# Chunked attention into a mixture of experts on one core: an earlier load of the second pair's first q and k, and another order of its softmax steps

## The chip, the cores and the metric

The kernel runs on one core of a Trainium2 chip. The metric is the device time of one execution, in microseconds (us); 1496.49 us is the median of three runs before the change. An engine executes its own instructions in the order of its own queue: TensorE (PE in the profile, PEld for its weight loads), VectorE (DVE), ScalarE (ACT), GpSimd (POOL) and SyncE (SP), which in this kernel issues every DMA. Engines wait for each other by semaphores.

## What is computed

The reference has two parts, and the second reads what the first writes:

```python
# attention inside chunks of 64 positions (8 batches, 8 heads, 576 positions, head_dim 64)
scores = scale * np.matmul(q_c, k_c.transpose(0, 1, 2, 4, 3))
scores = scores - np.max(scores, axis=-1, keepdims=True)
attn = np.exp(scores)
attn = attn / (np.sum(attn, axis=-1, keepdims=True) + 1e-09)
out = np.matmul(attn, v_c)
# the result as 4608 tokens of 512, through 4 experts of 512 -> 1024 -> 512
p = domain_probs / (domain_probs.sum(-1, keepdims=True) + 1e-09)
for e in range(E):
    h = np.maximum(x @ w1[e], 0.0)
    out += p[:, e:e + 1] * (h @ w2[e])
```

All of it is in fp32; the kernel splits each factor of the expert products into a high and a low part of type fp32r and adds three products of parts.

## The kernel before

The 4608 tokens are nine blocks of 512. The first block is worked alone, the other eight as four pairs of blocks. A pass takes one block or pair through half of one expert (512 of the 1024 hidden columns), so there are eight passes to each block or pair and 40 in all, numbered n = 0 to 39. Pass 0 is `startup`, passes 1 to 7 are `plain_pass`, pass 8 is `first_later_pass`, passes 9 to 39 are `later_pass`. The products of a pair follow a scheme with seven products in place of eight (`Group`, `LaterGroup`, `Outer`, L742 to L954). In `later_pass` a pass has 28 steps, listed in `WOVEN`; each step is one product of six matmuls of 128x512 on PE. Steps named g and h make hidden values of this pass; steps named a and b multiply the hidden values of the pass before with the second weight matrix. The products a1, a6, a7, a4 accumulate in one PSUM bank, and after each of them DVE adds the bank to an accumulator in SBUF (L923); the next product of the bank waits for that add. b1, b6, b7, b4 do the same after them, in the same bank.

What happens beside the products is written out by hand: `add(at, i, f)` puts f behind step i (counted from 0), and everything is emitted in this order, so the order in the code is the order in each engine's queue. The attention of a pair is done during the passes of the pair before it, two tiles of 128 tokens (t and t + 1) at a time. For the second pair `attend_second` does it, in passes 8 to 13:

- `both_load` (L248) loads q and k of two tiles into the tile hf3, two DMAs of 512 KB. The first call is in the last plain pass (n = 7, step 6, L1450), the others at step 26 of passes 9 to 11. In pass 7 the stores `keep(0)` (L488) read the former content of hf3.
- `two_next` multiplies weights and v of the two tiles before (L228) and makes the scores of the next two (L209, 64 matmuls of 64x64), at step 5 in passes 10 to 12 and at step 1 in pass 8.
- `a_softmax` is, for one tile, the maximum and its subtraction on DVE (L263, L268) and the exponential on ACT (L274).
- `two_weights` is five DVE instructions: the sums (L277), a small constant (L278), the reciprocal (L280), the scaling (L284) and a transpose in 32x32 blocks (L155).
- `a_place` is five copies on ACT (L161, L165), which put the transposed blocks in place.
- `two_load_v` loads v of the two tiles.

Other work that DVE does beside it: the hidden values (L896, L861), sums of hidden values for the seven products (L867, some on POOL), and sums of parts of the first weight matrix (L513). ACT and POOL make high parts (L873, L530) and low parts (L876, L531).

SP's queue holds the loads of weights for a ring of buffers (`ring_load`, L588), stores (L460, L488, L534, L1001), loads of raw weights (`half_load`, L508), and the loads named above. A DMA waits in this queue until its buffer is free and until the DMA eight places ahead of it has landed.

Of the kernel before, what the change touches and what calls it, by code (L numbers as in the profile page):

```python
# [18 lines left out]
NT = SUB // P  # L19
# [6 lines left out]
PAIR = 2  # L26
# [5 lines left out]
def chunk_attention_moe(ctx: ExitStack, tc: tile.TileContext, qk, v, v0, dp, w1, w2, out):  # L32
# [105 lines left out]
    def a_less_max(t):  # L138
        less_max(st[t]["sc"])

    def a_exps(t):
        a_exp(st[t]["sc"])

    def a_softmax(t):
        a_less_max(t)
        a_exps(t)

    def a_scale(t):

        s = st[t]  # L150
        s["e"] = att.tile([P, 2, HG, C], F32, name="e")
        scale(s["e"], s["sc"], s["r"])

    def a_transpose(t):
        nc.vector.transpose(st[t]["sc"], st[t]["e"])  # L155

    def a_place(t, name="pt"):

        s = st[t]
        s["pt"] = att.tile([P, 2, HG, C], F32, name=name)  # L160
        nc.scalar.copy(out=s["pt"], in_=s["sc"])  # L161
        for half in range(2):
            for i in range(2):
                here, there = (slice(half * C + k * B, half * C + (k + 1) * B) for k in (i, 1 - i))
                nc.scalar.copy(  # L165
                    out=s["pt"][there, :, :, i * B : (i + 1) * B],
                    in_=s["sc"][here, :, :, (1 - i) * B : (2 - i) * B],
                )
# [42 lines left out]
    def two_sums(t, name=None):  # L211
        z = bank(name)[:, : 2 * HG].rearrange("p (c j) -> p c j", c=2)
        st[t]["r"] = inverse_sums(st[t]["sc"], z)

    def two_weights(t):
        two_sums(t, "B1")
        a_scale(t)
        a_transpose(t)
# [29 lines left out]
    def both_load(t):  # L248

        both = hf_tile(3, (2, 2, 2, HG, C), F32)  # L250
        for i in range(2):
            st[t + i] = {"x": both[:, i]}
            nc.sync.dma_start(out=both[:, i], in_=qk[t + i].rearrange("g c d x h s -> (c d) g x h s"))
# [91 lines left out]
    def hf_tile(j, shape=(2, 2, SUB), dtype=F32R):  # L345

        return hpool.tile([P, *shape], dtype, name=f"hf{j}")

    def of_pass(w, n):
        return w[n % n_pass // 2, n % 2]  # L350
# [146 lines left out]
    def pieces(i, n):  # L497
        return scratch[0][:, SUB + 2 * i * P : SUB + 2 * (i + n) * P].rearrange(
            "p (a b c) -> p a b c", b=2, c=P
        )  # L500

    def half_load(n, g, fs=(0, 1)):
        if not scratch:
            scratch.append(xpool.tile([P, NK * PAIR * SUB], F32, name="xraw"))
        for f in fs:
            cols = slice((2 * f + g) * P, (2 * f + g + 1) * P)
            to = pieces(7 * g + AT[f"a{f + 1}1"], 2)
            nc.sync.dma_start(out=to.rearrange("p a b c -> p (a b) c"), in_=of_pass(w1, n)[:, :, cols])  # L508
# [390 lines left out]
    class Outer:  # L899
# [17 lines left out]
        def add(self, src, i, s):  # L917
            key = self.n // n_pass, 2 * i + self.g + NK * s
            if key not in acc:
                acc[key] = opool.tile([P, SUB], F32, name=f"acc{key[1]}")  # L920
                nc.scalar.copy(out=acc[key], in_=src)
            else:
                nc.vector.tensor_tensor(out=acc[key], in0=src, in1=acc[key], op=ALU.add)  # L923
# [456 lines left out]
    def plain_pass(n, beside, xs):  # L1380

        at, last_pass = {}, n == n_pass - 1
# [64 lines left out]
        for r, i in ((0, 2), (1, 2), (2, 3), (3, 5), (4, 5)):  # L1447
            add(at, i, lambda r=r: ring_load(0, r, (RINGS[0] + RINGS[1])[r]))
        add(at, 1, lambda: probs_load(n + 1, 0), lambda: probs_load(n + 1, 1))
        add(at, 6, lambda: half_load(n + 2, 0), lambda: both_load((1 + PAIR) * NT))  # L1450
        add(at, 6, lambda: ring_load(0, 5, RINGS[1][2]))
        issue(steps[:-1], at, beside, True)
        return steps[-1], w2_do("keep_sums")
# [82 lines left out]
    def attend_second(at, n):  # L1536

        t0, r = (1 + PAIR) * NT, n - n_pass - 1
        t = t0 + 2 * max(r, 0)
        if r < 0:  # L1540
            add(at, 1, lambda: two_next(None, t))
            add(at, 2, lambda: a_softmax(t))
            add(at, 3, lambda: two_weights(t), lambda: a_less_max(t + 1))
            add(at, 5, lambda: a_exps(t + 1))
            add(at, 7, lambda: a_place(t))
            return
        if r > 4:
            return
        if r:
            add(at, 5, lambda: two_next(t - 2, t if r < 4 else None, ("B1", "C0")))  # L1550
        if r == 4:
            return
        if r:
            add(at, 6, lambda: a_softmax(t))
            add(at, 12, lambda: two_weights(t))
            add(at, 13, lambda: a_softmax(t + 1))
            add(at, 15, lambda: a_place(t))
        for i in range(2):
            for odd in range(2):
                add(at, (7 if r else 14) + 2 * i + odd, lambda i=i, odd=odd: two_load_v(t + i, i, odd))  # L1560
        add(at, 18, lambda: two_weights(t + 1))
        add(at, 22, lambda: a_place(t + 1, "e"))
        if r < 3:
            add(at, 26, lambda: both_load(t + 2))

# [76 lines left out]
    def later_pass(n, ahead, late, held):  # L1642
# [39 lines left out]
        if 0 < pair < n_pairs - 1:  # L1682
            attend_two(at, pair + 1, n % n_pass)
        elif pair == 0:
            attend_second(at, n)
# [206 lines left out]
```

## Time and profile before

| what | us |
|---|---|
| median of three runs | 1496.49 |
| the three runs | 1496.47, 1496.91, 1496.49 |
| the profiled execution: its own time | 1496.58 |
| the profiled execution: its span, first to last instruction | 1494.5 |
| busy in the span: PE, DVE, POOL, ACT | 1463.3, 1080.8, 975.1, 624.1 |

Three stretches of the span, from the view that sums busy time by stretch (us):

| stretch | length | PE | DVE | POOL | ACT |
|---|---|---|---|---|---|
| 232.1 to 275.9 (pass 9) | 43.8 | 42.90 | 37.15 | 39.23 | 25.19 |
| 370.4 to 418.2 (pass 12) | 47.8 | 42.88 | 36.80 | 32.42 | 21.21 |
| 456.3 to 494.4 (a pass without attention) | 38.1 | 38.10 | 27.78 | 34.95 | 16.51 |

The profile is one execution. Its timeline merges equal instructions that follow each other; a bracket at a row's end gives the idle time of that engine before the row and what ended it. The granted clock of PE is 1.00 at 2.4 GHz and 0.50 at 1.2 GHz. Some matmul records can be missing, and the ends of matmuls are modelled. A wait for several semaphores is put down to the one that came last.

### The profile page before, as it was taken

The page shows a single profiled execution, that of the slowest core. Times are in us where ns is not written, and L with a number is a line of the kernel's source. Part 1 is how long each engine was busy: PE and PEld are TensorE (multiplying, and loading weights), DVE is VectorE, ACT ScalarE, POOL GpSimd, SP SyncE. Part 2 cuts the span into 40 slices and gives each one's busy share as a digit, 9 for nine tenths or more (in the row PEclk, how much of TensorE's full clock was granted, in tenths as well). Part 3 has the DMA queues.
Part 4 walks back from the last instruction along what each step waited for, and adds up shares of the span by engine and source line. Part 5 has one row for each costly group of instructions (what it writes and reads, how often), then busy time and mean ns, then how long its engine had stood idle before and what let it go on. Part 6 is the DMA issues. An engine that isn't in the chain of part 4 may idle for free.

```text
span 1494.5 us, 23390 instructions
## 1 busy us (share of the span) xinstructions
PE 1463.3 (98%) x8574; PEld 1203.3 (81%) x8574; DVE 1080.8 (72%) x1500; ACT 624.1 (42%) x1169; POOL 975.1 (65%) x728
## 2 busy tenths in 40 slices
PE   9999979988899999999999999999999999999998
PEld 7888867776688888888888888888888888888887
DVE  6666738787778797778766886777768866666666
ACT  5566525444444343444432434444333343333232
POOL 6878858776679875555555755555657655555554
PEclk9999989999999999999999999999999999999999
DMA  9899676856667879776655679676565696565655
GB/s 317 319 334 327 228 283 222 283 204 218 243 213 244 298 241 259 246 240 235 202 196 192 219 218 290 225 233 204 193 198 197 202 258 204 192 207 191 205 195 155
DMA packets 198418, 348.51 MB, mean 233 GB/s; under 512 B 70160, under 2 KB 109344, under 8 KB 197920
## 3 DMA queue, kind: packets, MB, share of 16 engines
q1 hardware_dynamic: 198304, 347.02, 70.6%
q8 instruction: 68, 1.11, 0.3%
q14 instruction: 46, 0.38, 0.1%
HBM read 275.59 MB, written 71.38 MB: 232 GB/s over the span
## 4 chain that ended last, share of the span: by engine, by line
PE 88%; DVE 4%; POOL 3%; DMA 2%; ACT 1%; issue 1%; SPq 0%; POOLq 0%; ACTq 0%; DVEq 0%
PE A L698 46%; PE C L698 25%; PE B L698 14%; POOL hf L876 2%; PE psa L209 1%; PE B L228 1%; DMA hf<-in_qk 1%; DMA v_in<-in_v 1%; DVE wraw L867 1%; DVE xraw L513 1%; POOL hf L388 0%; DMA w<-hf 0%; DVE acc L923 0%; DVE e L284 0%; POOL wraw L867 0%
## 5 line engine op out<-in xcount | busy, mean ns | idle before, releaser
L876 POOL TENSOR_TENSOR hf<-wraw,hf 128x512 fp32r<-128x512 f32 x384 | 505.6, 1334 | 254.2 <-ACT hf L873 251.1
L698 PE MATMUL A<-hf,wf 128*128 128x512 f32 x1536 | 395.4, 393 | 14.5 <-DVE acc L923 14.5
L698 PE MATMUL A<-xh,wf 128*128 128x512 f32 (+1 forms) x1120 | 388.2, 390 | 0.0
L698 PEld LDWEIGHTS A<-hf,wf 128*128 128x128 f32 x1536 | 286.6, 188 | 79.8 <-DVE acc L923 20.3
L873 ACT CAST hf<-wraw 128x512 fp32r<-128x512 f32 x384 | 233.4, 622 | 278.5 <-DVE wraw L867 98.0
L698 PEld LDWEIGHTS A<-xh,wf 128*128 128x128 f32 x1120 | 210.7, 188 | 45.0 <-POOL wf L531 0.5
L761 ACT COPY s<-A 128x512 f32<-128x512 f32 x192 | 112.8, 587 | 299.4 <-PE A L698 298.7
L698 PE MATMUL A<-xl,wf 128*128 128x512 f32 (+1 forms) x560 | 218.0, 389 | 0.0
L923 DVE TENSOR_TENSOR acc<-A,acc 128x512 f32<-128x512 f32 x232 | 157.9, 681 | 76.5 <-PE A L698 76.2
L698 PE MATMUL C<-xh,wf 128*128 128x512 f32 (+1 forms) x584 | 201.1, 388 | 1.0 <-DVE B L896 1.0
L698 PE MATMUL C<-hf,wf 128*128 128x512 f32 x768 | 195.6, 390 | 0.0
L698 PEld LDWEIGHTS C<-hf,wf 128*128 128x128 f32 x768 | 145.0, 189 | 30.3
L698 PEld LDWEIGHTS C<-xh,wf 128*128 128x128 f32 x584 | 109.4, 188 | 24.0 <-DVE B L896 1.4
L867 POOL TENSOR_TENSOR wf<-wraw,wf 128x512 f32<-128x512 f32 x31 | 40.1, 1294 | 133.5 <-DVE wf L861 131.8
L876 POOL TENSOR_TENSOR hf<-wf,hf 128x512 fp32r<-128x512 f32 x64 | 89.9, 1405 | 51.8 <-ACT hf L873 51.8
L698 PEld LDWEIGHTS A<-xl,wf 128*128 128x128 f32 x560 | 105.7, 189 | 22.0
L698 PE MATMUL B<-xh,wf 128*128 128x512 f32 (+1 forms) x344 | 115.4, 384 | 0.0
L923 DVE TENSOR_TENSOR acc<-C,acc 128x512 f32<-128x512 f32 x120 | 82.6, 688 | 45.3 <-PE C L698 43.0
L698 PE MATMUL C<-xl,wf 128*128 128x512 f32 (+1 forms) x292 | 113.2, 388 | 0.0
L867 DVE TENSOR_TENSOR wraw<-wf,wraw 128x512 f32<-128x512 f32 x64 | 96.6, 1510 | 11.2 <-POOL hf L876 10.0
L698 PE MATMUL B<-hf,wf 128*128 128x512 f32 x384 | 97.7, 389 | 0.0
L867 POOL TENSOR_TENSOR wraw<-wraw 128x512 f32<-128x512 f32 x63 | 93.5, 1485 | 0.0
(253 smaller groups left out, 1994.0 us busy)
## 6 DMA issues: line engine op xcount, KB each, us to landing
wf<-w SPq DMA_DIRECT2D x402, 512.0 KB, 4.2
w<-wf SPq DMA_DIRECT2D x46, 512.0 KB, 5.1
w<-hf SPq DMA_DIRECT2D x28, 512.0 KB, 6.5
w<-hf SPq DMA_DIRECT2D x42, 256.0 KB, 5.2
wf<-in_w SPq DMA_DIRECT2D x19, 512.0 KB, 6.2
xraw<-in_qk SPq DMA_DIRECT2D x14, 512.0 KB, 7.7
qk_in<-in_qk SPq DMA_DIRECT2D x12, 512.0 KB, 6.4
ws<-p_t SPq DMA_DIRECT2D x24, 256.0 KB, 4.2
```

Of the source, the lines that this page charges most:

```text
L209: nc.tensor.matmul(s["sc"][of_half(half), c, slot], lhsT=q, rhs=k, start=True, stop=True)
L228: nc.tensor.matmul(av[half][of_half(slot % 2), i, head // 2], lhsT=s["v"][of_half(half), head // 2, head % 2], rhs=s["pt"][of_half(half), ...
L513: (eng or nc.vector).tensor_tensor(out=to, in0=a, in1=b, op=op)
L698: nc.tensor.matmul(out, lhsT=lhs(k, a), rhs=rhs(k, b), start=first and i == 0, stop=last and i == len(parts) - 1, skip_group_check=not (fi ...
L761: nc.scalar.copy(out=t, in_=self.a)
L867: (eng or nc.vector).tensor_tensor(out=self.values[place, k], in0=self.values[a, k], in1=self.values[b, k], op=op)
L873: nc.scalar.copy(out=self.part(name, 0)[:, k], in_=self.values[name, k])
L876: (eng or nc.gpsimd).tensor_tensor(out=self.part(name, 1)[:, k], in0=self.values[name, k], in1=self.part(name, 0)[:, k].bitcast(F32), op=A ...
L923: nc.vector.tensor_tensor(out=acc[key], in0=src, in1=acc[key], op=ALU.add)
```

## The change

Two things are changed. In pass 7 the call of `both_load` moves from step 6, behind `half_load`, to step 3. In `attend_second` the softmax steps move: for the first tile of two, in passes 10 to 12, `two_weights` goes from step 12 to 8 and `a_place` from 15 to 12; the second tile's `a_softmax` goes from 13 to 12, behind that `a_place`; in passes 9 to 12 the second tile's `two_weights` goes from 18 to 17 and its `a_place` from 22 to 20. No instruction is added or removed.

```diff
@@ plain_pass @@
-        add(at, 6, lambda: half_load(n + 2, 0), lambda: both_load((1 + PAIR) * NT))
+        add(at, 3, lambda: both_load((1 + PAIR) * NT))
+        add(at, 6, lambda: half_load(n + 2, 0))
@@ attend_second @@
         if r:
             add(at, 6, lambda: a_softmax(t))
-            add(at, 12, lambda: two_weights(t))
-            add(at, 13, lambda: a_softmax(t + 1))
-            add(at, 15, lambda: a_place(t))
+            add(at, 8, lambda: two_weights(t))
+            add(at, 12, lambda: a_place(t), lambda: a_softmax(t + 1))
@@ attend_second @@
-        add(at, 18, lambda: two_weights(t + 1))
-        add(at, 22, lambda: a_place(t + 1, "e"))
+        add(at, 17, lambda: two_weights(t + 1))
+        add(at, 20, lambda: a_place(t + 1, "e"))
```

On SP at the end of pass 7, before (hf is the tile of the kept products in L488 and that of q and k in L253; wf is the ring of weights, acc an output tile of pass 7, xraw raw weights):

```order
L588 DMA wf_2461<-w_0_2_99 128x1024
L1001 DMA out<-acc_551 128x512
L488 DMA w_1_2_190<-hf_2429 128x1024
L488 DMA w_1_5_193<-hf_2429 128x1024
L1001 DMA out<-acc_552 128x512
L588 DMA wf_2505<-w_0_3_100 128x1024
L588 DMA wf_2507<-w_0_4_101 128x1024
L1001 DMA out<-acc_553 128x512
L508 DMA xraw<-in_w 128x4x128 x2
L253 DMA hf_2527<-in_qk 128x2x512 x2
```

And in the changed kernel:

```order
L588 DMA wf_2461<-w_0_2_99 128x1024
L253 DMA hf_2463<-in_qk 128x2x512 x2
L1001 DMA out<-acc_551 128x512
L488 DMA w_1_2_190<-hf_2429 128x1024
L488 DMA w_1_5_193<-hf_2429 128x1024
```

The two loads of q and k now stand ahead of nine other DMAs, from the first store of an output tile to the two half loads, and no longer behind them.

On DVE in pass 11 (pass 12 reads the same), behind the add of step 8, a3 (psa holds the scores, B_37.. and C_3741 banks of the hidden values):

```order
 L923 TENSOR_TENSOR acc_2866<-C_3643,acc_2866 128x512
-L896 TENSOR_TENSOR B_3771<-C_3741,s_3772 128x512
-L861 SCALAR_TENSOR_TENSOR wraw<-B_3771,ws 128x512
+L277 TENSOR_REDUCE B_3759<-psa 128x8
+L278 TENSOR_SCALAR B_3759<-B_3759 128x8
+L280 RECIPROCAL z_3762<-B_3759 128x8
+L284 TENSOR_TENSOR e<-psa,z_3762 128x512
+L155 STREAM_TRANSPOSE psa<-e 128x2x256
+L896 TENSOR_TENSOR B_3779<-C_3741,s_3780 128x512
+L861 SCALAR_TENSOR_TENSOR wraw<-B_3779,ws 128x512
```

The five instructions of `two_weights` now stand ahead of g7's hidden values.

On DVE in the same pass, around the add of step 13, a4 (acc_2936):

```order
-L861 SCALAR_TENSOR_TENSOR wf_3812<-C_3741,ws 128x512
-L277 TENSOR_REDUCE B_3815<-psa 128x8
-L278 TENSOR_SCALAR B_3815<-B_3815 128x8
-L280 RECIPROCAL z_3818<-B_3815 128x8
-L284 TENSOR_TENSOR e<-psa,z_3818 128x512
-L155 STREAM_TRANSPOSE psa<-e 128x2x256
+L861 SCALAR_TENSOR_TENSOR wf_3820<-C_3741,ws 128x512
+L263 TENSOR_REDUCE m_3829<-psa 128x8
+L268 TENSOR_TENSOR psa<-psa,m_3829 128x2x256
 L923 TENSOR_TENSOR acc_2936<-A_3586,acc_2936 128x512
-L263 TENSOR_REDUCE m_3830<-psa 128x8
-L268 TENSOR_TENSOR psa<-psa,m_3830 128x2x256
```

Ahead of a4's add stood five instructions for the first tile, and now two for the second.

## Rows read from the trace of the kernel before

**Rows 1.** PE's waits, whole span: line, waited for; us in total, times, longest.

```profile
PE A L698 <- DVE acc L923: 14.5, 9, 2.3
PE psa L209 <- DMA hf<-in_qk: 9.4, 2, 9.2
```

**Rows 2.** PE's timeline, pass 8: start, us, what, count, idle before and its end.

```profile
211.30 1.18 PE L209 MATMUL psa<-hf 64*64 64x64 f32 x32 [9.22 <-DMA hf<-in_qk]
```

**Rows 3.** The chain that ended last: start, us, what and count.

```profile
49.22 5.44 PE C L698 x24
...
213.83 4.75 PE C L698 x12
```

**Rows 4.** PE's timeline, pass 12: the scores of two tiles.

```profile
379.63 1.17 PE L209 MATMUL psa<-hf 64*64 64x64 f32 x64
```

**Rows 5.** SP's timeline, end of pass 7: start, time to issue, what, count.

```profile
188.23 1.25 SPq L488 DMA_DIRECT2D w<-hf  x2
...
191.90 1.48 SPq L588 DMA_DIRECT2D wf<-w  x3
196.17 0.34 SPq L1001 DMA_DIRECT2D out<-acc  x1
...
198.87 2.29 SPq L588 DMA_DIRECT2D wf<-w  x2
...
203.46 1.88 SPq L253 DMA_DIRECT2D hf<-in_qk  x2
```

**Rows 6.** DMAs issued near 188.9, near 192.9 and at 204.4: KB each, us to landing.

```profile
w<-hf SPq DMA_DIRECT2D x2, 512.0 KB, 5.3
...
wf<-w SPq DMA_DIRECT2D x2, 512.0 KB, 7.9
...
hf<-in_qk SPq DMA_DIRECT2D x1, 512.0 KB, 8.1
```

**Rows 7.** PE's timeline, waits in passes 9 (first), 10 (next two) and 12.

```profile
271.73 1.66 PE L698 MATMUL A<-hf,wf 128*128 128x512 f32 x6 [0.91 <-DVE acc L923]
...
302.32 2.37 PE L698 MATMUL A<-hf,wf 128*128 128x512 f32 x6 [1.93 <-DVE acc L923]
...
314.23 1.66 PE L698 MATMUL A<-hf,wf 128*128 128x512 f32 x6 [1.82 <-DVE acc L923]
...
396.40 1.66 PE L698 MATMUL A<-hf,wf 128*128 128x512 f32 x6 [1.77 <-DVE acc L923]
...
401.61 1.66 PE L698 MATMUL A<-hf,wf 128*128 128x512 f32 x6 [0.83 <-DVE acc L923]
...
408.31 2.52 PE L698 MATMUL A<-hf,wf 128*128 128x512 f32 x6 [2.32 <-DVE acc L923]
```

**Rows 8.** Busy time by stretch, every engine; then PE's granted clock, DMA share, GB/s.

```profile
408.73:412.14 3.41, 3.41 (x10) 2.65 (x9) 3.41 (x6) 1.19 (x3) 1.76 (x3) 0.51 0.49 165
```

**Rows 9.** DVE's timeline, pass 12.

```profile
387.19 0.70 DVE L896 TENSOR_TENSOR B<-C,s 128x512 f32<-128x512 f32 x1 [1.34 <-ACT s L761]
...
393.15 0.69 DVE L277 TENSOR_REDUCE B<-psa 128x8 f32<-128x512 f32 x1
...
395.68 0.67 DVE L923 TENSOR_TENSOR acc<-A,acc 128x512 f32<-128x512 f32 x1
...
398.83 0.70 DVE L896 TENSOR_TENSOR B<-B,s 128x512 f32<-128x512 f32 x1 [1.15 <-ACT s L761]
...
400.88 0.68 DVE L923 TENSOR_TENSOR acc<-A,acc 128x512 f32<-128x512 f32 x1
...
403.37 1.76 DVE L867 TENSOR_TENSOR wraw<-wf,wraw 128x512 f32<-128x512 f32 x1 [1.22 <-POOL hf L876]
```

**Rows 10.** POOL's busy time during step 21's three L513 on DVE, passes 9, 12.

```profile
267.30:271.00 3.70, 3.49 (x3) 1.00 0.74 240
408.97:410.90 1.93, 1.00 (x1) 0.50 0.50 202
```

**Rows 11.** DVE's waits, whole span.

```profile
DVE m L263 <- ACT pt L165: 15.1, 8, 1.9
```

## Prediction

> **What bounds the kernel now.** PE does: its waits add up to little, and outside them one product follows the other. So I read the view of PE's waits first, for the whole span. It has two entries of weight [rows 1]: nine waits for the adds on DVE, 14.5 us together, and one place that waits 9.4 us for q and k. The change touches both. Next I read PE's timeline around each wait, then the queue that ends it: SP's for the load, DVE's for the adds. The reader should see that PE's idle time is in two places only, pass 8 and passes 9 to 12, and that each wait of over 1.9 us is paid twice, since the granted clock falls to 0.50 around or after it.
>
> **The load, part one.** PE finishes the step before the scores at 211.30 - 9.22 = 202.08 and starts them at 211.30 [rows 2]. SP issued the two loads only from 203.46 [rows 5], with PE already waiting, and the second took 8.1 us to land [rows 6].
>
> Where it goes: its new place is behind the three ring loads issued from 191.90 to 193.4. It now waits for the two stores that read hf3, issued at 188.23 and about 188.9 [rows 5]; the second lands 5.3 us later [rows 6], at 194.2. So the loads issue at about 194.2 and 194.7, nine us sooner. The next DMA in SP's queue stores an output tile and issued at 196.17 before [rows 5], so the hold keeps nothing behind it waiting.
>
> When it lands: I take the DMAs to land in the order of issue. The last ring load, issued near 192.9, lands 7.9 us later at 200.8 [rows 6]. The two halves of q and k came 1.3 us apart before: the first ended PE's wait at 211.30 [rows 2], the second landed at 204.4 + 8.1 = 212.5. So they land at 202.1 and 203.4. PE wants the first at 202.08 and the second 0.6 us later: a wait of 0.8 us is left. Bounds: no wait, if they land in 5.3 us like the stores; 2.5 us, if a transfer ahead is late by two such halves.
>
> The Trainium skill (DMA: Bandwidth & Descriptors, Queues, rings and completion order) says that descriptors are consumed in ring order but that completion isn't FIFO, so that a later DMA may finish first. By that rule the wait left could be nil and the sum 0.8 us better; no row here shows one DMA overtaking another.
>
> What goes with it: after the stall the scores ran at half clock, two halves of 1.18 us [rows 2] where 64 such matmuls take 1.17 [rows 4], and the twelve matmuls after them took 4.75 against 2.72, half of 5.44 [rows 3]. With a wait of 0.8 us I take it that the clock stays: of the nine waits for DVE, only the three of 1.93 us and more were followed by 0.50. So the gain is 9.4 - 0.8 + 1.2 + 2.0 = **11.8 us**. Bounds: 12.6 with no wait; 6.9 with 2.5 us left and the low clock still paid.
>
> What is pushed back: two ring loads for pass 8 stand behind it, issued from 198.87 [rows 5]. With the 7.9 us of the loads before them [rows 6] and two halves, 2.6 us, for the megabyte now ahead, they land near 209.4 and 210.7. Their products, h1 and h2, come after the scores (done at 202.08 + 0.8 + 1.2 = 204.1), a product of twelve matmuls and three of six (2.7 + 4.1 us), so at 210.9 and 212.2. Both are in time by 1.5 us. The half loads land later too, but POOL, which sums them, starts only once PE has gone on.
>
> Everything behind this place is paced by PE, so I let the 11.8 us stand to the end.
>
> **The order on DVE, part two, passes 11 and 12.** I retime pass 12; pass 11 has the same three waits. In pass 12 PE waits 1.77 us before b1, 0.83 before b6, 2.32 before b7 [rows 7], each for the add of the product before in the same bank.
>
> - Step 8: DVE stands idle 1.34 us until 387.19 [rows 9]. `two_weights` takes 395.68 - 393.15 = 2.53 us [rows 9]. From 385.85 it ends at 388.4, so the work that began at 387.19 begins 1.2 us late. That work lasts to 393.15, and now to 394.3.
> - Step 12: then comes the second tile's maximum and subtraction, 1.4 us by the 0.69 of a like DVE pass [rows 9], to 395.7. a4's add comes then, where it was at 395.68. Nothing is won at b1: of the 2.5 us taken out ahead of this add, 1.2 come back as lateness and 1.4 as the two instructions put in. Part of b1's wait moves to a4, since a7's add is 1.2 us late too.
> - Step 15: h2's hidden value started at 398.83, held by ACT, whose copy stood behind the second tile's exponential. The subtraction now ends at 395.7 and not 2.0 us later, so this starts at 396.8, and b1's add is at 398.8, not 400.88 [rows 9]. The 0.83 us before b6 goes.
> - Step 17: `two_weights` of the second tile now runs from 400.1 to 402.6, in time in which DVE partly stood idle for POOL (1.22 us to 403.37) [rows 9]. The 1.76 us sum follows, to 404.4, then b6's add, to 405.0. b7 waits for it and starts at 405.0, not 408.31: 3.3 us. Six products of 1.36 us behind b1's 396.4 it could start at 404.5, so some 0.6 us of its wait is left.
> - The clock: the low stretch after b7 lasts 3.41 us at half rate [rows 8], worth 1.7 us. The waits left are about 0.8 at a4, 1.0 at b1 and 0.6 at b7, so I take it as gone.
> - Step 21, a cost: the three sums L513 stand ahead of b7's add, which b4 waits for. They took 1.93 us with POOL busy for 1.00 of it in pass 12, and 3.70 with POOL busy for 3.49 in pass 9 [rows 10], where b4 did wait 0.91 [rows 7]. Three us sooner they fall beside POOL's low parts. I take the price of pass 9, 0.85 us, not nil.
>
> The Trainium skill (GPSIMD Engine Reference, Specifications) states that GpSimd shares its SBUF interfaces with VectorE and contends with DVE instructions that have two SBUF inputs, as L513 has. The two rows of L513 agree; without that rule the sum would be 0.85 us a pass better.
>
> So passes 11 and 12 give 3.3 + 1.7 - 0.85 = 4.1 each, **8.2 us**. Bounds: 1 a pass if the waits only move and the clock still falls; 5.5 if also the L513 cost nothing.
>
> **Passes 10 and 9.** Pass 10 waits 1.93 us at b1, with the low clock after it, and 1.82 at b7 [rows 7]. By the same steps nothing is won at b1 itself, the low stretch goes (1.7), b7's wait falls to 0.6 (1.2), and b4 pays 0.85: **2.1 us**, between 0 and 3. In pass 9 only the second tile moves: as in pass 12, `two_weights` goes into time in which DVE stood idle for POOL, and I take b7's add to come early enough to end b4's 0.91 us: **0.9 us**, or nil.
>
> The moved `a_place` copies cost ACT nothing, as it is busy under half of these passes. But at step 12 they stand ahead of the second tile's maximum, and where the kernel has that order now DVE's maximum waits for the copies: eight times, up to 1.9 us each [rows 11]. Here the transpose that they read ends at 388.4 and DVE comes to the maximum at 394.3, which leaves them 5.9 us, so I price it at nil; its upper end is 1.9 a pass, 5.7 us.
>
> **The sum.** 11.8 + 8.2 + 2.1 + 0.9 = 23.0 us. The profiled execution took 1496.58, 2.1 of it outside the 1494.5 span, and lies 0.1 above the median of 1496.49. So 1496.5 - 23.0 = **1473.5 us**.
>
> **The rivals.**
>
> - The load still lands late: the eight-place rule and the bandwidth ahead of it leave 2.5 us or more, and the clock falls as now. For it: DMAs issued there took 7.9 and 8.1 us, where one a little earlier took 5.3 [rows 6]. Against it: nine us of lead. Part one gives 6.9: 1478.
> - The waits only move: DVE is busy 36.80 of a pass, and what leaves b1 appears at a4 and b4, in one piece long enough to lower the clock. Part two gives 4 in place of 11.2: 1481. For it: b1 wins nothing even by my own sum.
> - Better than the forecast: no wait at the load, no price for L513, shorter waits at b1: 12.6 + 11 + 3 + 0.9 = 27.5, about 1469.
> - Slower than before: DVE's maximum at step 12 waits for the copies, and these stand on ACT behind a cast that waits for a store's landing. Each us beyond 394.3 holds a4's add and so PE. It decides where the copies end 8 us later than that, about 402, in each of three passes: that eats 24 us, and 1498 comes out. Against it: the longest such wait now is 1.9 us [rows 11].
> - The change doesn't do what it says: hf3 isn't free before PE needs it, and the load stays where it was. The waits of rows 5 and 6 speak against it; with part two alone 1485.
>
> **How the numbers follow.** Forecast 0.55, late load 0.13, moved waits 0.14, better 0.11, slower 0.03, load unmoved 0.02, and 0.02 for no net effect. The range takes in the late load, the moved waits with 1.5 us over them, and the better case with 1 us under it for a shorter wait at b1: 1468 to 1482.5. A change under 0.2% (3 us) can't be told from none. Faster: 0.95, same 0.02, slower 0.03.
>
> **What would show it.** Right: L253 issued near 194 to 195 on SP; PE's wait for q and k under 2 us and the clock at 1.00 there; in passes 10 to 12 no low stretch after b7, no wait at b6, small new ones at a4 and b4. Wrong: PE waiting at h1 for a ring load; DVE's maximum waiting for L165 in passes 10 to 12; a wait at a4 of over 2 us; a low clock after any of them.

## The result and the profile after

The changed kernel takes 1471.6 us (median of four executions, 1470.21 to 1474.14) against 1496.7 us before (1496.47 to 1496.95): a ratio of 0.9834, with a 95% interval from 0.9817 to 0.9851. The forecast was 1473.5 us, with 1468 to 1482.5 as its range. The profiled execution took 1470.92 us, its span is 1469.1.

The answer to [rows 1] is the same view of PE's waits in the changed kernel (line, waited for; us in total, times, longest). The nine waits for the adds, 14.5 us together, are six of at most 0.7, and the 9.4 us for q and k are 1.4:

```profile
PE A L698 <- DVE acc L923: 3.7, 6, 0.7
PE psa L209 <- DMA hf<-in_qk: 1.4, 2, 0.8
```

To [rows 5] and [rows 2] answer SP's timeline at the end of pass 7 (start, time to issue, what, count) and PE's at the scores of pass 8, both of the changed kernel. L253 is issued at 195.26, with the output tile behind it at 196.75 as foreseen. PE still waits for either half, and the scores run at full rate:

```profile
188.80 1.27 SPq L488 DMA_DIRECT2D w<-hf  x2
...
192.53 1.41 SPq L588 DMA_DIRECT2D wf<-w  x3
195.26 1.03 SPq L253 DMA_DIRECT2D hf<-in_qk  x2
196.75 0.36 SPq L1001 DMA_DIRECT2D out<-acc  x1
```

```profile
203.86 0.74 PE L209 MATMUL psa<-hf 64*64 64x64 f32 x32 [0.82 <-DMA hf<-in_qk]
205.17 0.74 PE L209 MATMUL psa<-hf 64*64 64x64 f32 x32 [0.57 <-DMA hf<-in_qk]
```

To [rows 7] and [rows 9] answer PE's and DVE's timelines of pass 12 in the changed kernel. Two waits are left there, at a4 and at b1, and no half clock behind them. A third shows on PE's weight loads alone (PEld, the last line of the first block): at g6 of pass 13 they wait 0.50 us for POOL's L531, and the next product begins 1.72 us after g6 and not 1.36 as before. On DVE the sum L867 takes 0.67 us in place of 1.76, and the three sums L513 2.83:

```profile
371.26 1.66 PE L698 MATMUL A<-hf,wf 128*128 128x512 f32 x6 [0.52 <-DVE acc L923]
...
376.36 1.66 PE L698 MATMUL A<-hf,wf 128*128 128x512 f32 x6 [0.70 <-DVE acc L923]
...
398.96 0.30 PEld L698 LDWEIGHTS A<-xh,wf 128*128 128x128 f32 x2 [0.50 <-POOL wf L531]
```

```profile
375.62 0.68 DVE L923 TENSOR_TENSOR acc<-A,acc 128x512 f32<-128x512 f32 x1
377.03 0.70 DVE L896 TENSOR_TENSOR B<-B,s 128x512 f32<-128x512 f32 x1 [0.73 <-ACT s L761]
...
382.82 0.67 DVE L867 TENSOR_TENSOR wraw<-wf,wraw 128x512 f32<-128x512 f32 x1
383.41 0.67 DVE L923 TENSOR_TENSOR acc<-A,acc 128x512 f32<-128x512 f32 x1
...
384.79 2.83 DVE L513 TENSOR_TENSOR xraw<-xraw 128x256 f32<-128x256 f32 x3
387.55 0.68 DVE L923 TENSOR_TENSOR acc<-A,acc 128x512 f32<-128x512 f32 x1
```

For the comparison of runs one mark serves: the first product L228 of a pass (the attention in its sixth step) on PE's timeline. A pass is the time from its mark to the next one's, so its start holds all that came before, the load with it. From pass 13's mark to the end every run takes 1067.6 to 1068.3 us, so nothing is given back later.

| kernel | median us (low to high) | before beside it | mark of pass 10 | passes 10, 11, 12 |
|---|---|---|---|---|
| before | 1496.7 | | 284.19 | 46.63, 47.82, 47.82 |
| changed | 1471.6 (1470.2 to 1474.1) | 1496.7 | 273.24 | 42.72, 42.75, 42.75 |
| changed, a second time | 1471.79 (1470.3 to 1472.9) | 1496.8 | 272.47 | 42.73, 42.77, 42.73 |
| load alone | 1486.65 (1484.6 to 1489.9) | 1496.8 | 275.92 | 48.22, 47.84, 47.83 |
| steps alone | 1481.06 (1479.4 to 1482.8) | 1496.8 | 281.71 | 43.35, 42.79, 42.72 |
| load, first tile's steps | 1473.95 (1472.5 to 1475.5) | 1496.8 | 273.15 | 43.21, 43.19, 43.23 |
| load, second tile's steps | 1480.36 (1480.1 to 1480.5) | 1496.8 | 271.90 | 46.56, 46.20, 46.18 |
| maximum one step later | 1473.05 (1473.0 to 1476.1) | 1496.8 | 271.96 | 43.81, 43.82, 43.81 |
| first weights two steps later | 1474.51 (1472.7 to 1476.3) | 1496.8 | 274.83 | 44.49, 43.67, 43.69 |
| first copies three steps later | 1473.73 (1473.2 to 1477.8) | 1497.8 | 272.02 | 44.16, 44.15, 44.19 |
| load, first copies alone | 1485.04 (1483.9 to 1486.7) | 1496.8 | 274.88 | 47.29, 46.92, 46.92 |
| load ahead of a ring load | 1468.70 (1468.6 to 1469.8) | 1496.8 | 270.80 | 42.73, 42.75, 42.71 |
| and sums in the fifth step | 1465.91 (1465.6 to 1466.2) | 1497.8 | 271.12 | 41.62, 41.88, 41.89 |
| and sums in two places | 1462.54 (1462.3 to 1463.3) | 1496.8 | 270.79 | 40.81, 40.78, 40.76 |

### The profile page after: what moved, and what is told of

It reads as the page before. It is cut to its first block, busy times and chain, and to the rows that moved or that the text cites. A ratio compares the mean times of both kernels' runs of the same rounds, so it can differ in the third digit from the quotient of the medians.

```text
span 1469.1 us, 23388 instructions
## 1 busy us (share of the span) xinstructions
PE 1456.3 (99%) x8574; PEld 1198.4 (82%) x8574; DVE 1079.3 (73%) x1500; ACT 624.2 (42%) x1169; POOL 975.8 (66%) x728
## 4 chain that ended last, share of the span: by engine, by line
PE 73%; POOL 1%; DVE 0%; DMA 0%; issue 0%; ACT 0%; POOLq 0%; DVEq 0%
PE A L698 41%; PE C L698 20%; PE B L698 10%; PE psa L209 1%; PE B L228 1%; POOL hf L876 0%; DMA wf<-w 0%; POOL wf L531 0%; PE C L228 0%; DVE xraw L513 0%; POOL wraw L867 0%; DVE acc L923 0%; ACT e L165 0%; PE C L1802 0%; PE psa L698 0%
## 5 line engine op out<-in xcount | busy, mean ns | idle before, releaser
L923 DVE TENSOR_TENSOR acc<-A,acc 128x512 f32<-128x512 f32 x232 | 157.9, 681 | 77.3 <-PE A L698 76.8
L698 PE MATMUL C<-hf,wf 128*128 128x512 f32 x768 | 194.8, 389 | 0.0
L867 POOL TENSOR_TENSOR wf<-wraw,wf 128x512 f32<-128x512 f32 x31 | 40.1, 1295 | 133.5 <-DVE wf L861 132.8
L923 DVE TENSOR_TENSOR acc<-C,acc 128x512 f32<-128x512 f32 x120 | 82.6, 688 | 47.0 <-PE C L698 43.2
L867 DVE TENSOR_TENSOR wraw<-wf,wraw 128x512 f32<-128x512 f32 x64 | 93.5, 1461 | 5.5 <-POOL hf L876 4.4
L867 POOL TENSOR_TENSOR wraw<-wraw 128x512 f32<-128x512 f32 x63 | 94.1, 1493 | 0.0
```

The lines of the kernel that those rows point to most:

```text
L698: nc.tensor.matmul(out, lhsT=lhs(k, a), rhs=rhs(k, b), start=first and i == 0, stop=last and i == len(parts) - 1, skip_group_check=not (fi ...
L867: (eng or nc.vector).tensor_tensor(out=self.values[place, k], in0=self.values[a, k], in1=self.values[b, k], op=op)
```

## The two parts apart

**The load alone.** The softmax steps stand as before, the load is moved.

```diff
-            add(at, 8, lambda: two_weights(t))
-            add(at, 12, lambda: a_place(t), lambda: a_softmax(t + 1))
+            add(at, 12, lambda: two_weights(t))
+            add(at, 13, lambda: a_softmax(t + 1))
+            add(at, 15, lambda: a_place(t))
...
-        add(at, 17, lambda: two_weights(t + 1))
-        add(at, 20, lambda: a_place(t + 1, "e"))
+        add(at, 18, lambda: two_weights(t + 1))
+        add(at, 22, lambda: a_place(t + 1, "e"))
```

> Only the load is moved; the weights and the copies stand in passes 9 to 12 as before. Parts that only add up: the scores of pass 8 begin 9.7 us earlier than in the kernel before, as in the changed kernel, and nothing else changes, so 1496.6 - 9.7 = 1487 us; passes 10 to 12 keep their waits at b1 (1.9, 1.8, 1.8), b6 and b7 (1.8, 2.3, 2.3) and the three stretches of 3.4 us at half clock, and last 46.6, 47.8 and 47.8 us. Rival, the parts help each other: an earlier and even entry into pass 9 shortens waits of passes 10 to 12 by itself, they last under 47 us, and the time is 1484 or less.

1486.65 us: 10.2 us faster, and the passes 11 and 12 are as long as before. So the load doesn't help them; the rival falls. Pass 10 is not as expected: it lasts 48.22 us and not 46.63. PE's timeline of it, against the two rows of pass 10 in [rows 7]:

```profile
294.05 1.65 PE L698 MATMUL A<-hf,wf 128*128 128x512 f32 x6 [1.92 <-DVE acc L923]
299.26 1.66 PE L698 MATMUL A<-hf,wf 128*128 128x512 f32 x6 [0.84 <-DVE acc L923]
305.96 1.74 PE L698 MATMUL A<-hf,wf 128*128 128x512 f32 x6 [2.33 <-DVE acc L923]
```

The half clock follows the third wait here, at b7, and not the first, at b1. Yet b7 begins 30.04 us after the pass's mark in both (314.23 before, 305.96 here). With the half clock behind b1 PE only waits less for DVE at b6 (not at all) and at b7 (1.82 us). Behind b7 no such wait follows, and there the half clock makes the pass 1.6 us longer.

The four executions spread over 5.3 us. The slowest of them is the profiled one. A part of its delay is that pass; another part is seen on PE's timeline at the scores: the second half came 1.72 us late, the scores after it took 1.18 us in place of 0.74, and the twelve matmuls behind them 4.00, where the changed kernel's profile has 3.02 from 205.84 on.

```profile
202.72 0.74 PE L209 MATMUL psa<-hf 64*64 64x64 f32 x32 [0.65 <-DMA hf<-in_qk]
205.19 1.18 PE L209 MATMUL psa<-hf 64*64 64x64 f32 x32 [1.72 <-DMA hf<-in_qk]
206.31 4.00 PE L698 MATMUL C<-hf,hf 128*128 128x512 f32 x12
```

**The steps alone**, the load as before:

```diff
-        add(at, 3, lambda: both_load((1 + PAIR) * NT))
-        add(at, 6, lambda: half_load(n + 2, 0))
+        add(at, 6, lambda: half_load(n + 2, 0), lambda: both_load((1 + PAIR) * NT))
```

> Only the steps of passes 9 to 12 are moved; the load stands where it did. Parts that add up: PE waits some 9.3 us for q and k in pass 8, the granted clock falls to 0.50 after that, and the passes 9 to 12 gain what they did in the changed kernel, 1.2 + 4.2 + 5.1 + 5.1 = 15.6 us: 1481 us. Rival, the gain of passes 9 to 12 hangs on the load: 1484 or more, with a wait of over 1.9 us or a low clock left in one of passes 10 to 12.

1481.06 us, 15.7 us faster. PE waits 9.28 and 0.17 us for q and k and runs the scores at half clock, as before; the passes 11 and 12 are as short as with the load, pass 10 is 0.6 us longer. The parts add up: 10.2 + 15.7 = 25.9 against 25.1 for both, a difference within the spread of the executions.

## Which step earned the passes

**The first tile's steps alone, and the second's alone**, both with the load moved. The first puts 17 and 20 back to 18 and 22, the second puts the three lines of the first tile back, each as in the diff above.

> The load moved, and the first tile's steps alone (its weights in the ninth step, its copies and the second tile's maximum in the 13th); the second tile's weights back in the 19th step, its copies in the 23rd. The two tiles' moves overlap: DVE comes out of b1's add 2 us earlier, the sum L867 and then the second tile's weights end by about 384.5 on the clock of the changed kernel's pass 12, b6's add half a us behind that, so b7 waits 0.5 to 1 us and no low clock follows; 1472.5 to 1475 us. Rival, each tile's move earns its own part, as the forecast counted the 3.3 us at b7 to the second tile's weights: b7 waits near 2 us, with the low clock behind it, and the time is 1479 us or more.

> The load moved, and the second tile's steps alone (its weights in the 18th step, its copies in the 21st); the first tile's weights in the 13th step, the maximum in the 14th, its copies in the 16th. The moves overlap: the second tile's weights fill the time in which DVE stood idle for POOL, so the wait at b7 (1.8 in pass 10, 2.3 in 11 and 12) and the low clock after it go, 1.8 + 4.0 + 4.0 us, while the waits at b1 (1.8 to 1.9) and b6 (0.8) stay and in pass 10 the low clock after b1 with them: 1471.6 + 15.6 - 1.2 - 9.8 = 1476 us. Rival, without the first tile's move DVE comes too late: b7 still waits over 1 us and the time is 1479 us or more.

The first tile's moves give 4.6 of the 5.1 us of a pass (47.82 to 43.2), with 0.48 us left at b7, and 1473.95 us; the theory held. The second tile's give 1.6 (47.82 to 46.2): my theory missed that by 4 us, and the rival's numbers hold, 1480.4 us. Its low clock behind b7 went, but b7 still waits 1.05 (0.56 in pass 11, where a half clock fell behind b1 and the pass was no longer for it), and early in the next pass a wait came that neither theory had. PE's timeline of pass 12 in that run:

```profile
382.41 1.66 PE L698 MATMUL A<-hf,wf 128*128 128x512 f32 x6 [1.77 <-DVE acc L923]
387.63 1.65 PE L698 MATMUL A<-hf,wf 128*128 128x512 f32 x6 [0.84 <-DVE acc L923]
393.05 1.65 PE L698 MATMUL A<-hf,wf 128*128 128x512 f32 x6 [1.05 <-DVE acc L923]
...
408.35 0.73 PE L698 MATMUL A<-xh,wf 128*128 128x512 f32 x2 [0.85 <-POOL wf L531]
```

The last row is a wait for POOL, which splits the weights for the next pass. So POOL's queue is late when DVE's is. In pass 9, where only the second tile moves, its step is worth 1.25 us: the marks of pass 10 in these two runs, 273.15 and 271.90, with the same waits for q and k (0.6 and 0.6).

**The maximum one step later**, behind a4's add:

```diff
-            add(at, 12, lambda: a_place(t), lambda: a_softmax(t + 1))
+            add(at, 12, lambda: a_place(t))
+            add(at, 13, lambda: a_softmax(t + 1))
```

> The changed kernel with the second tile's maximum one step later, in the 14th step and so behind a4's add on DVE. Theory, the first tile's weights in the ninth step are what earned the time, since they fill 1.34 us in which DVE stood idle, and DVE is full from there to b1: the wait at b1 (0.70) goes, a wait of 0.4 to 0.7 comes at b6, since h2's hidden value comes 0.6 us later, and a pass lasts 42.4 to 42.75 us as against 42.72: 1470.6 to 1471.6 us. Rival, the earlier maximum earned it: b6 waits 0.8 us and b7 over 1 us again, a pass lasts over 43.5 us, 1474 us or more.

Neither. A pass takes 43.81, 1.1 us more. The wait at b1 goes and 0.69 comes at b6, as the theory said; but PE also waits 0.80 for POOL's L531 at the next pass, as in the run before. The step isn't free: counted from pass 11's mark, h2's hidden value on DVE (334.69 here, 334.29 in the changed kernel, whose mark is 0.2 later), POOL's first sum of h (336.50 and 336.11) and L867 (340.48 and 340.08) all come 0.6 us later, and POOL's L531 for the next pass comes 1.1 later (355.33 and 354.42), as much as the pass is longer.

**The first tile's weights two steps later:**

```diff
-            add(at, 8, lambda: two_weights(t))
+            add(at, 10, lambda: two_weights(t))
```

> The changed kernel with the first tile's weights two steps later, in the 11th step and so behind a7's add and its neighbours on DVE. Theory, what the ninth step earned is the 1.34 us in which DVE waited for ACT's copy of s: DVE stands idle again, a4 waits no more, b1 waits 0.7 + 0.5 + 1.3 = 2.0 to 2.5 us in place of 0.70, and the low clock may come back behind it; a pass lasts 43.5 to 46 us, 1474 to 1481 us. Rival, the step within this stretch doesn't matter since DVE has to do the same work before b1: the wait moves from a4 to b1 (1.2 us), a pass lasts 42.7 us, 1471.6 us.

A pass takes 43.68, 0.95 more; 1474.5 us. DVE stands idle for ACT's copy of s again, by the 1.34 us of [rows 9], and PE waits 2.3 us in place of 1.22. The size is what the theory said; the place isn't. The long wait is at h1, for the bank A that L861 still has to read on DVE, behind the weights. In pass 10 it was 1.80 us, a half clock followed it, and the pass lasts 44.49. DVE's and PE's timelines of that run's pass 12:

```profile
371.53 0.70 DVE L896 TENSOR_TENSOR B<-C,s 128x512 f32<-128x512 f32 x1 [1.34 <-ACT s L761]
...
377.19 0.67 DVE L861 SCALAR_TENSOR_TENSOR wraw<-A,ws 128x512 f32<-128x512 f32 x1
```

```profile
377.92 0.50 PE L698 MATMUL A<-xh,wf 128*128 128x512 f32 x1 [1.65 <-DVE wraw L861]
381.57 1.66 PE L698 MATMUL A<-hf,wf 128*128 128x512 f32 x6 [0.64 <-DVE acc L923]
```

**The first tile's copies back in the 16th step**, nothing else:

```diff
-            add(at, 12, lambda: a_place(t), lambda: a_softmax(t + 1))
+            add(at, 12, lambda: a_softmax(t + 1))
+            add(at, 15, lambda: a_place(t))
```

> The changed kernel with the first tile's copies alone put back into the 16th step; the second tile's maximum stays in the 13th. Theory, the copies cost nothing in either place, since ACT has idle time in both: passes of 42.7 us, 1471.6 us; on DVE the maximum comes at the same time. Rival, their place matters: behind the second tile's exponential and the copy of s they hold ACT's later casts, from which POOL's chain hangs, and PE waits for POOL as where the maximum came a step later: 43.3 us or more a pass, 1473.5 us or more.

The rival holds: 44.17 us a pass, 1.43 more. This is the edit that the prediction priced at nil. The chain can be read off the timeline of all engines in pass 11, first in this run, then in the changed kernel, with b1 at nearly the same time in both (333.82 and 333.61):

```profile
335.33 1.49 ACT L165 COPY pt<-psa 32x256 f32<-32x256 f32 x4
336.85 1.14 ACT L873 CAST hf<-wraw 128x512 fp32r<-128x512 f32 x2
...
337.55 2.54 POOL L876 TENSOR_TENSOR hf<-wraw,hf 128x512 fp32r<-128x512 f32 x2 [1.37 <-ACT hf L873]
340.06 1.28 POOL L531 TENSOR_TENSOR wf<-xraw,wf 128x512 fp32r<-128x512 f32 x1
...
340.11 1.78 DVE L867 TENSOR_TENSOR wraw<-wf,wraw 128x512 f32<-128x512 f32 x1
```

```profile
335.32 1.14 ACT L873 CAST hf<-wraw 128x512 fp32r<-128x512 f32 x2 [0.55 <-PE A L698]
...
336.11 2.74 POOL L876 TENSOR_TENSOR hf<-wraw,hf 128x512 fp32r<-128x512 f32 x2
338.80 1.29 POOL L531 TENSOR_TENSOR wf<-xraw,wf 128x512 fp32r<-128x512 f32 x1
...
340.08 0.67 DVE L867 TENSOR_TENSOR wraw<-wf,wraw 128x512 f32<-128x512 f32 x1
```

With the copies ahead of them, ACT's casts come 1.53 us later, POOL starts 1.44 later, and its L531 now runs just when DVE comes to L867. Beside it L867 takes 1.78 us, alone 0.67. That holds b6's add by 1.1 us, b7 waits 0.27, and POOL's chain, late by the rest, makes PE wait 0.81 in the next pass.

**The first tile's copies alone**, on the run with the load alone:

```diff
-            add(at, 12, lambda: two_weights(t))
+            add(at, 12, lambda: two_weights(t), lambda: a_place(t))
             add(at, 13, lambda: a_softmax(t + 1))
-            add(at, 15, lambda: a_place(t))
```

> The kernel with only the load moved, and of the steps of passes 10 to 12 one alone: the first tile's copies go from the 16th to the 13th step, behind its weights and ahead of the second tile's exponential on ACT. Theory, the copies' place is a part of its own, through ACT's casts, POOL's sums of h and the sum L867 that waits for POOL: ACT's casts come some 1.4 us earlier, b7's wait falls from 2.3 to about 1.1 and the low clock behind it goes, while b1 (1.8) and b6 (0.8) wait as before: 44.9 us a pass in place of 47.8, 1478 us. Rival, the place of the copies only counts once DVE's work is early: less than 1 us a pass, 1484 us or more.

The rival: 46.92 against 47.84 us, 0.9 a pass, 1485.0 us. b7's wait did fall to 1.09, but the second tile's maximum now stands on DVE right behind the copies that ACT has only just been given, and waits for them. DVE's waits over the span of that run, against [rows 11], then its timeline in pass 12:

```profile
DVE m L263 <- ACT pt L165: 19.9, 11, 1.9
```

```profile
388.40 0.69 DVE L263 TENSOR_REDUCE m<-psa 128x8 f32<-128x512 f32 x1 [1.60 <-ACT pt L165]
```

This is the mechanism of the prediction's slower rival at work, three times 1.6 us. In the changed kernel that view reads as in [rows 11], 15.1 us and eight times: with the weights in the ninth step the copies are long done when DVE comes to the maximum. L867 still takes 1.76 us beside POOL, and PE waits up to 1.1 us at b6 in place of 0.8. So the move of the copies is worth 1.43 us a pass where the weights are early and 0.9 where they are not. The weights and the maximum were not run alone.

## What was left, and a faster kernel

**The changed kernel again**, to see its scatter beside the others:

> The changed kernel itself, beside the others on one chip. Theory, its times scatter because the second half of q and k comes at the edge: in its longer executions PE waits over 1.5 us for that half and the scores and the product behind them run at half clock, which costs 2.9 us: 1470.2 to 1474.2 us, the granted clock of the longer ones lower. Rival, the scatter comes from elsewhere: the profiled execution shows the same 1.4 us at the scores whatever its time.

1471.79 us (1470.28 to 1472.86). The profile fell on its fastest execution, with 1.06 and 0.59 us at the scores, so it can't tell the theories apart. Two profiles of other kernels with the same load can in part: the slowest execution of the load alone (above) had 1.72 us and half clock, and one of the run with the weights two steps later, 1476.21 us where that kernel's best took 1472.74, had 1.82 us and half clock. That supports the theory, but both profiles have a half clock in pass 10 too. And another execution of the second kernel took 1476.34 us at a mean granted clock of 1.00, so the half clock isn't all of it. Where the rest of the scatter comes from stays open.

**The load ahead of the third ring load:**

```diff
+        add(at, 3, lambda: both_load((1 + PAIR) * NT))
         for r, i in ((0, 2), (1, 2), (2, 3), (3, 5), (4, 5)):
...
-        add(at, 3, lambda: both_load((1 + PAIR) * NT))
```

> The changed kernel with its load of q and k one place further ahead, in front of the third ring load. Theory, the queue is full and bytes land in the order of issue: with half a megabyte less ahead, at some 400 GB/s, the two halves land 1.3 us sooner after the same issue (near 195.3), so the two waits of 0.6 to 0.8 us at the scores go and the half clock that some executions show behind the second of them too; 1.4 us off the best executions of the changed kernel, nearly 3 more off its worst: 1469 to 1470 us, all within 1.5 us. The ring load now comes 2.6 us later, near 203.5, before the end of the scores. Rival, latency and not order sets the landing: both waits stay at 0.6 to 0.8, 1471.6 us. Second rival, the product that reads the third ring load waits for it instead, over 1 us: 1472 us or more.

1468.70 us (1468.59 to 1469.84): 0.3 us under the theory's range, and the scatter is down to 1.3 us. No wait at the scores, and none for the ring load. How long the two halves took to land, first in the changed kernel, then here; then the scores on PE's timeline here; last two stretches of the changed kernel (busy time of PE, PEld, DVE, ACT, POOL; granted clock, share of the DMA engines, GB/s):

```profile
DMA to landing us min/median/max: 8.6/9.0/9.4
```

```profile
DMA to landing us min/median/max: 6.5/6.9/7.4
```

```profile
202.26 1.21 PE L209 MATMUL psa<-hf 64*64 64x64 f32 x64
```

```profile
198.00:202.00 4.00, 3.89 (x18) 2.92 (x17) 1.70 (x3) 0.30 (x1) 3.92 (x3) 1.00 1.01 404
202.00:206.00 4.00, 2.62 (x70) 1.90 (x69) 1.39 (x2) 0.28 (x1) 3.61 (x3) 1.00 1.04 405
```

They land 2.1 us sooner after their issue. 1.3 us of that is what half a megabyte takes at the 404 to 405 GB/s of these stretches, in which the 16 DMA engines are full by the share shown; the rest lies ahead of them, as the first ring load too landed sooner here (6.2 us after its issue, 7.4 in that profile of the changed kernel). In both the first half lands 1.3 us behind the DMA issued before it (202.51 and 203.81, 199.71 and 201.06), so the place in the queue sets the landing. The Trainium skill (DMA: Bandwidth & Descriptors, Queues, rings and completion order) lets a later DMA finish before an earlier one. No run here shows that: in every profile the DMAs of SP's queue land in the order of their issue, as far as it has their landings, and as the prediction took it.

**The sums L513 in the fifth step**, on top of it, in passes 10 to 12:

```diff
-            half_sums(first, 1, (5, 6, 11, 12) if n == n_pass + 1 else (9, 9, 10, 11))
+            half_sums(first, 1, (5, 6, 11, 12) if n == n_pass + 1 else (4,) * 4 if n < n_pass + 5 else (9, 9, 10, 11))
```

> The kernel with the load ahead of the third ring load, and in passes 10 to 12 four more instructions moved on DVE: the four sums L513 of the next factors, in the tenth to 12th step so far, go to the fifth, where DVE stood idle 2.97 us waiting for the attention's products. Theory, DVE's queue is what is left of the waits: two us less ahead of a4's add, so neither a4 (0.52) nor b1 (0.70) waits, a pass lasts 41.5 us in place of 42.73, and 1468.7 - 3.7 = 1465 us. Rival, POOL is next: its sum L531 for the first products of the next pass, which came with no margin, holds PE 0.5 to 1.2 us a pass: 1466.5 to 1468.7 us, no more than half of the gain.

1465.91 us. The waits at a4 and b1 are gone: they were DVE's queue. But 41.9 us a pass isn't 41.5: one wait of 0.53 came at the product that needs the bank C, which the add behind the four sums frees. DVE's timeline of pass 12, and the busy time of that stretch, the fifth after the comma POOL's:

```profile
354.48 5.13 DVE L513 TENSOR_TENSOR xraw<-xraw 128x256 f32<-128x256 f32 x4
359.53 0.68 DVE L923 TENSOR_TENSOR acc<-C,acc 128x512 f32<-128x512 f32 x1
```

```profile
354.48:359.61 5.13, 5.13 (x141) 4.18 (x140) 5.10 (x6) 1.71 (x5) 5.13 (x5) 1.00 0.41 128
```

POOL was busy for all of it, and each sum took 1.28 us. The gap of 2.97 us that I had read as room for four sums of 0.42 wasn't that.

**Two sums in the fifth step and two in the eighth:** `(4, 4, 7, 7)` in place of `(4,) * 4`.

> The kernel with the load ahead of the third ring load and the four sums L513 moved, now two of them in the fifth step and two in the eighth, where DVE waits another 0.72 us for the first tile's exponential. Theory, four sums in a row were 0.5 us too long for the first gap and made the one wait left (0.28, 0.54, 0.53 us); two fit each gap, PE doesn't wait in passes 10 to 12, a pass lasts 41.35 us: 1465.9 - 1.3 = 1464.6 us. Rival, the sums in the eighth step only push the wait to a4 or b1: 1465.5 to 1466.5 us.

1462.54 us, 2 us better than the theory, with no wait in PE's view of passes 10 to 12: 40.78 us a pass. (The wait of 0.72 us in the eighth step, which I put down to the exponential, ends with a product of PE in bank C by the profile.) Against the kernel before the ratio is 0.9774, interval 0.9759 to 0.9788. The same two views show two sums beside POOL and two without it:

```profile
352.23 2.25 DVE L513 TENSOR_TENSOR xraw<-xraw 128x256 f32<-128x256 f32 x2
...
358.08 0.75 DVE L513 TENSOR_TENSOR xraw<-xraw 128x256 f32<-128x256 f32 x2
```

```profile
352.23:354.48 2.25, 2.25 (x130) 2.04 (x129) 2.21 (x4) 0.89 (x4) 2.25 (x3) 1.00 0.19 71
358.08:358.83 0.75, 0.75 (x5) 0.63 (x4) 0.75 (x3) 0.57 (x2) 0.05 (x1) 1.00 1.14 341
```

## Why the prediction held, and where it didn't

The time came out 1.9 us under the forecast, from a load that gave 1.6 us less and steps that gave 4.5 more. The mechanisms were right in the main, but a part of the closeness is luck, since these two errors stand against each other.

**The load, 11.8 us.** Alone it gave 10.2, its executions 6.9 to 12.2 (1496.8 less the highest and the lowest). That the lowest is the bound of 6.9 is luck: in that execution 1.6 us were lost in pass 10. There are nine profiles with the load in this place. Up to the first product behind the scores that waits for DVE in each of them (226.35 before), they come 8.1 to 11.0 us sooner.

Where the load goes was right: eight of the nine issue it at 194.2 to 194.8. The 195.26 above belongs to an execution in which PE too reached the scores a us later, at 203.04. That the halves land in the order of issue, some 1.3 us behind what is ahead of them, that the loads behind them come in time, and that the output tile isn't held, was right as well. (In three of the nine one of the ring loads or halves landed 2.5 to 2.8 us behind the one before it; what held it stays open.) Two terms were mis-sized:

- The landing. The 7.9 us taken for the last ring load are the median of two [rows 6]; that load itself took 8.2, and in the nine profiles 7.9 to 9.5. The halves landed 8.0 to 9.5 and 8.9 to 10.4 us after their issue, where 7.9 and 8.7 were worked out. The wait left is 0.9 to 2.4 us in all, not 0.8. It is 2.4 in the three profiles just named, and in two of these a half clock came with it.
- The half clock. It was worth 2.7 us from the scores to that product, not 1.2 + 2.0.

**The steps, 11.2 us for passes 9 to 12.** Alone they gave 15.7; pass by pass, in the profiles, 1.25 + 3.9 + 5.1 + 5.1. Pass 12, counted from its mark, step by step (before the mark is at 378.64, after at 358.71):

- b1: "nothing is won": right. It begins 17.76 us after the mark before and 17.65 now. The wait of 1.77 is split into 0.52 at a4 and 0.70 at b1, near the 0.8 and 1.0 foreseen.
- b6: its wait is gone, as said; it begins at 22.97 before, at 21.88 now.
- b7: 3.3 foreseen, 3.7 measured (29.67 to 25.96), and no wait is left where 0.6 was foreseen. The reason given was wrong in part. I had the second tile's weights in the 18th step earn it; the run without that step loses 0.5 us only.
- "The 1.76 us sum follows": here the term fails. L867 takes 0.67, as POOL is done by then. It is done because the copies no longer stand on ACT ahead of the casts that feed it. So the sentence that the moved copies "cost ACT nothing" asked the wrong question: ACT has idle time in either place, but what stands behind the copies in its queue is not idle. Their move is worth 1.43 us a pass with the others, and was booked at nil with a loss as its only bound.
- The low clock behind b7: gone, and worth the 1.7 foreseen. From b7 to b4 it took 5.82 us and takes 4.08 now.
- The price for L513, 0.85: not paid. The three sums took 2.83 us, between the 1.93 and 3.70 of [rows 10], with POOL busy for 2.39 of them, and b7's add behind them ended at 388.2, half a us before b4 began at 388.75 without a wait.
- A term that the sum didn't have: the 0.36 us at g6 of the next pass, which now waits for POOL's L531.

So 3.3 + 1.7 - 0.85 = 4.1 should have been 3.71 + 1.74 - 0.36 = 5.09, and 5.07 us were measured.

In pass 10 the sum gave 2.1 and the passes 3.9, beyond its bound of 3. Here the clock's term was wrong in kind. The 1.7 us were booked for the half clock behind b1, but the run with the load alone shows that b7 begins at the same time without it, as DVE sets that time. What was won is DVE's alone: b7 begins 4.1 us sooner after the mark (30.04 to 25.94), where 1.2 were foreseen for it, again without a price for L513; 0.3 us of it go at g6. Pass 9's 0.9 was 1.25.

**The rivals.** The late load is not a case of its own but a share of the executions: a half clock at the scores in two of nine profiles. The waits moved in part, to a4 and b1 and 0.36 us to g6, with no half clock behind any of them. The better case, 1469, is where the kernel comes out once the load has no wait (1468.7). The slower mechanism is real, 1.6 us each time, where the copies move and the weights don't. That the load wouldn't move is refuted by its issue at 195.26.

## What to carry to other kernels

Price a moved instruction by what stands behind it in its own queue, on through the engines that wait for that, and not by whether its engine has idle time. Ask of each DVE instruction with two SBUF inputs what POOL does in that moment, since the same instruction may cost about three times as much. Book nothing for a slower PE ahead of a wait that another engine ends. A load that comes just in time can cost more than the wait of one profile shows. In eight of the nine sets of executions with the load in its new place the times spread over 2.6 to 5.3 us (0.45 in the ninth, with the second tile's steps), and over 0.7 to 1.3 in the three kernels with the load one place earlier. That the load causes the spread is not shown: with the load where it stood before, in the run with the steps alone, it was 3.5.

## What the runs showed of the hardware

**DVE beside POOL.** Sums of two SBUF operands: L867 (128x512) took 0.67 us with POOL busy for 0.01 us of it, and 1.76 [rows 9] with POOL busy throughout. L513 (128x256) took 0.37 us each with POOL all but idle, 1.28 each beside it, 3.5 times as long. The Trainium skill (GPSIMD Engine Reference, Specifications) states the contention and no size for it; these rows agree and give one. DVE's other passes of the shape 128x512 that read one operand from PSUM, as L923 and L277, kept 0.64 to 0.70. The size follows a simple pattern in the changed kernel's trace: all 114 L867 of this shape on DVE that begin with over 0.15 us of an instruction of POOL still to run end 0.55 to 0.56 us after that instruction's end, and all 23 such L513 0.28 to 0.29 us after it. So the price was what was left of POOL's instruction.

**A wait costs more than the profile shows as idle.** In the changed kernel a4 begins 2.16 us after the product ahead of it (369.10 to 371.26) and lasts 1.50 until the next begins; without the wait, in the last run, these are 1.48 and 1.38. A wait of 0.52 thus cost 0.80, and in the same way one of 0.70 cost 1.01. With 0.15 us less at g6 (1.72 to 1.57) that makes up the 1.95 us a pass that the last run gained from 1.22 us of waits.

**The half clock isn't told by the wait alone.** A wait of 1.93 us in pass 10 was followed by a granted clock of 0.50 before the change [rows 7], and one of 1.92 in the run with the copies alone; one of 1.92 with the load alone and one of 1.93 with the second tile's steps alone were not. A wait of 1.78 was followed by it in pass 11 of the second tile's run, and not in the same place before the change. Before the scores 1.72 and 1.82 us were followed by it, 1.80 in the run with the copies alone was not. The prediction's line at 1.93, drawn from nine waits, doesn't hold; what decides in these cases stays open.

**The half clock costs time only where PE sets the pace.** Behind b7 before the change it cost 1.7 us. Behind b1, with waits for DVE at b6 and b7 still to come, it cost nothing: b7 begins 30.04 us after the mark with it and without it. In the run with the second tile's steps alone pass 11 has it behind b1 and pass 12 doesn't, and they last 46.20 and 46.18 us; with the copies alone both last 46.92.
